# Attention of the x queries: steps of four heads, outputs of one unit beside the score gradients of the preceding unit, TensorE order fixed by hand

## Chip, core and metric

The kernel runs on one core of a Trainium2 chip. The metric is the device time of one execution in microseconds (us), as the median of several executions. The program before takes 9416.67 us (three executions, 9407.48 to 9422.91).

## The reference, cut to what matters

The program computes a forward value and eleven gradients of a gated mixture of two attention branches, `out = g*a + (1-g)*b`. Branch A is a 32-head attention of width 18 with one shared key and value. Branch B, in which the change lies, cuts 2048 tokens into 64 segments of 32; each segment attends to itself and to 8 memory rows, with 32 heads of width 128, and the first 8 output rows are the next segment's memory:

```python
for s in range(n_seg):
    xs = x[:, s * seg_len:(s + 1) * seg_len, :].copy()
    h = jnp.concatenate([mem, xs], axis=1)
    q = jnp.einsum('btd,dhe->bhte', h, Wq)
    ...
    scores = jnp.where(mask[None, None], scores, -1000000000.0)
    p = _softmax(scores, axis=-1)
    o = jnp.einsum('bhqk,bhke->bhqe', p, v)
    o = jnp.einsum('bhte,hed->btd', o, Wo)
    mem = o[:, :M, :].copy()
    outs.append(o[:, M:, :])
...
return g * a + (1 - g) * b
...
_out, _vjp = jax.vjp(_f, A_x, A_wq, ...)
_grads = _vjp(grad_out)
```

## The kernel before

The program works through stages, each of which opens and closes its own memory pools (`build_full`): branch A (`a_setup`, `a_attention`, `a_final`), the projections of all tokens (`b_project`), the serial forward chain of the memory rows (`b_chain_fwd`), the attention of the x queries (`b_x_attention`), the serial backward chain (`b_chain_bwd`), the gradients of x (`b_x_gradients`), and the gradients of the weights (`b_weight_gradients`). What one stage hands to a later one goes through DRAM.

`b_project` writes q, k and v twice: token by token (`XT`, tokens on partitions) and column by column (`XE`, the 128 elements of a head on partitions). In `XE` the heads of a half stand in the order i, g, where a head's number is 16 r + 4 g + i. For k and v it also writes `XS`, segment by segment (tile `p_seg`, copied on GpSimd).

`b_x_attention` is the stage of the change. It takes 16 tiles of 128 tokens (`tt`), and for each two halves of 16 heads (`r`): 32 units. For the 16 heads of a unit, with masks that keep each token to its own segment, it

- loads the key, query and value columns and rows (`x_ke`, `x_qe`, `x_ve`, `x_tv`, `x_tq`, `x_tk`, six transfers of 512 KB) and the memory columns (`x_me`, made on GpSimd of `raw_x_me`), and turns the latter into rows (`x_mk`, `x_mv`);
- takes the scores against the memory rows (L505 to L511: four heads share the array, each in 32 of its columns) and their exponentials `x_em` (ScalarE), then in four groups the scores against the tokens and the exponentials `x_et` (L519);
- sums them with one-column matmuls into `pl`, and takes the reciprocals `x_rl` on VectorE (L526);
- multiplies them with the values: for each head one matmul of all 128 rows with `x_tv`, and one of 32 rows (a quarter of the array) with `x_mv`, in turn (L532 to L535); VectorE scales the result to `x_ot` (L536), which is transposed to `x_oe` and projected with `WoN` into `pb`;
- makes the gradients of the outputs from `dbT` and `WoT` (`x_dot`, transposed to `x_doe`), in five matmuls, the last of which has 64 rows; multiplies them with `x_oe` on GpSimd (`x_pr`, L560);
- makes the gradients of the scores, `x_dsm` for the memory rows and `x_dst` for the tokens (L576, VectorE);
- transposes `x_et`, `x_dst`, `x_em` and `x_dsm` (`x_eq`, `x_sq`, `x_eqm`, `x_sqm`), sums over the memory rows (`x_dk`), and makes the gradients of the queries (`x_dq`): again one matmul of 128 rows with `x_tk` and one of 32 rows with `x_mk`, in turn (L604 to L606).

Every result goes back to DRAM in six transfers of 512 KB, three from the queue of SyncE (SP) and three from that of GpSimd (POOL), and eight small ones of `x_dk`. `pb` collects the projections of both halves of a token tile, and the tile ends with the gate's work on 576 columns (`x_bs`, `x_diff`, `x_out`, `dz_all`) and two one-row matmuls for the gradient of the gate.

The order of the instructions on each engine is set by a list scheduler, which may move them past each other; where `self.chain` is true, `follow` (L66) ties each TensorE instruction to the one before, and TensorE keeps the order in which the code is written. In this stage `chain` is false. Matmul results go into one pool of banks, `x_p` with four buffers, transposes into `x_tr` with two, `pb` takes two banks. Every matmul is recorded at L78 and every transpose at L83, inside the helpers `mm` and `tr`; copies out of transposes are at L62 (VectorE) or L64 (ScalarE).

Of the kernel before, what the change touches and what calls it, by code (L numbers as in the profile page):

```python
# [11 lines left out]
P = 128  # L12
# [17 lines left out]
class Kern:  # L30
# [3 lines left out]
    def __init__(self, tc, T, A_x, A_wq, A_wk, A_wv, A_wo, B_mem0, B_Wq, B_Wk, B_Wv, B_Wo,  # L34
# [19 lines left out]
        self.chain, self.last = False, None  # L54

# [158 lines left out]
    def b_project(self, keep, sp, psum):  # L214
# [6 lines left out]
        for tt in range(NTT):  # L221
            tok = slice(tt * P, (tt + 1) * P)
            for w in "kvq":
                tk = sp.tile([P, J], BF16, name="p_tok", bufs=2)
                te = sp.tile([P, 2, 4, 4, P], BF16, name="p_em", bufs=2)
                for c in range(8):
                    pb = psum.tile([P, 512], F32, name="p_pb", bufs=4)
                    for kt in range(NKT):
                        wap, rows = self.w_nat(w, kt, c * 512, (c + 1) * 512)
                        self.mm(pb[:, :], lhsT=xT[rows, kt, tok], rhs=wap, start=(kt == 0), stop=(kt == NKT - 1))  # L230
                    self.evac(tk[:, c * 512:(c + 1) * 512], pb[:, :])
                    ptr = psum.tile([P, 4, P], BF16, name="p_tr", bufs=3)
                    for i in range(4):
                        self.tr(ptr[:, i], tk[:, c * 512 + i * E:c * 512 + (i + 1) * E], P)
                    self.evac(te[:, c // 4, :, c % 4, :], ptr[:])
                nc.sync.dma_start(self.XT[w][tok, :], tk[:, :])
                nc.gpsimd.dma_start(self.XE[w][tt], te[:].rearrange("p r i g t -> p (r i g t)"))
                if w == "q":
                    continue
                for sl in range(4):  # L240
                    ts = sp.tile([P, 32, SEG], BF16, name="p_seg", bufs=2)
                    nc.gpsimd.tensor_copy(ts[:], te[:].rearrange("p r i g (s t) -> p (r i g) s t", s=4)[:, :, sl, :])
                    nc.gpsimd.dma_start(self.XS[w][4 * tt + sl], ts[:].rearrange("p h t -> p (h t)"))
# [162 lines left out]
    def load_WoT(self, pool, psum, WoN):  # L406

        t = pool.tile([P, NKT, J], BF16, name="WoT")
        for h4 in range(8):
            for kt in range(NKT):  # L410
                rows = KT_ROWS[kt]
                ptr = psum.tile([P, 4, P], BF16, name="x_tr", bufs=2)
# [7 lines left out]
    def load_em(self, sp, name, src, tt, r, bufs=2):  # L420

        t = sp.tile([P, 4, 4, P], BF16, name=name, bufs=bufs)
        self.nc.sync.dma_start(t[:].rearrange("p i g t -> p (i g t)"), src[tt][:, r * 2048:(r + 1) * 2048])
# [21 lines left out]
    def tr4(self, psum, name, src_fn, dst, use=None):  # L445

        ptr = psum.tile([P, 4, P], BF16, name="x_tr", bufs=2)
# [4 lines left out]
    def b_x_attention(self, keep, sp, psum, WoN, WoT):  # L452


        nc = self.nc
        NTT = self.NTT
        gwb = keep.tile([P, D], BF16, name="gwb")
        nc.sync.dma_start(gwb[:], self.gate_w.partition_broadcast(P))
        pdgs = keep.tile([1, D], F32, name="dgate_acc")
        for tt in range(NTT):  # L460
            tok = slice(tt * P, (tt + 1) * P)
            x = sp.tile([P, D], BF16, name="x_x", bufs=2)
            nc.sync.dma_start(x[:], self.A_x[tok, :])
            go = sp.tile([P, D], BF16, name="x_go", bufs=2)
            nc.sync.dma_start(go[:], self.grad_out[tok, :])
            at = sp.tile([P, D], BF16, name="x_a", bufs=1)
            nc.sync.dma_start(at[:], self.a_dram[tok, :])
            zc = sp.tile([P, 4], F32, name="x_z", bufs=2)
# [7 lines left out]
            gt, omg = zc[:, 2:3], zc[:, 3:4]  # L476
            db = sp.tile([P, D], BF16, name="x_db", bufs=2)
            nc.vector.tensor_scalar(out=db[:], in0=go[:], scalar1=omg, scalar2=None, op0=ALU.mult)
            nc.gpsimd.dma_start(self.db_dram[tok, :], db[:])
            dbT = sp.tile([P, NKT, P], BF16, name="x_dbT", bufs=2)  # L480
            for k4, n in ((0, 4), (4, 1)):
                ptr = psum.tile([P, 4, P], BF16, name="x_tr", bufs=2)
                for k in range(n):
                    rows = KT_ROWS[k4 + k]
                    self.tr(ptr[0:rows, k, :], db[:, (k4 + k) * P:(k4 + k) * P + rows], P)
                rows = KT_ROWS[k4]
                self.evac(dbT[0:rows, k4:k4 + n, :], ptr[0:rows, 0:n, :])
            pb = psum.tile([P, 640], F32, name="x_b", bufs=1)
            for r in range(2):
                qe = self.load_em(sp, "x_qe", self.XE["q"], tt, r)  # L490
                ke = self.load_em(sp, "x_ke", self.XE["k"], tt, r)
                ve = self.load_em(sp, "x_ve", self.XE["v"], tt, r, 1)
                hc = slice(r * 2048, (r + 1) * 2048)
                xt = {}
                for w in "vqk":
                    xt[w] = sp.tile([P, 4, 4, E], BF16, name=f"x_t{w}", bufs=1)
                    nc.sync.dma_start(xt[w][:].rearrange("p g i e -> p (g i e)"), self.XT[w][tok, hc])
                me = self.load_me(sp, "x_me", self.ME, (1, 2), tt, r)
                mk = self.tok_me(sp, psum, "x_mk", me, 0)
                mv = self.tok_me(sp, psum, "x_mv", me, 1)  # L500
                mes = lambda w, i, g: me[:, w, 4 * i + g, :]

                et = sp.tile([P, 4, 4, P], BF16, name="x_et", bufs=1)
                em = sp.tile([P, 4, P], BF16, name="x_em", bufs=1)
                Sm = psum.tile([P, 4, P], F32, name="x_p", bufs=4)  # L505
                self.mm(Sm[:].rearrange("p i n -> p (i n)"), lhsT=self.identB[:, :],
                        rhs=self.maskM[:].rearrange("p i n -> p (i n)"), start=True, stop=False)
                for i in range(4):
                    for g in range(4):
                        self.mm(Sm[32 * g:32 * g + 32, i, :], lhsT=mes(0, i, g), rhs=qe[:, i, g, :],  # L510
                                start=False, stop=True, tp=(0, 32 * g))  # L511
                nc.scalar.activation(em[:], Sm[:], ACT.Exp, scale=SCALEB)
                for i in range(4):
                    S = psum.tile([P, 4, P], F32, name="x_p", bufs=4)
                    self.mm(S[:].rearrange("p g n -> p (g n)"), lhsT=self.identB[:, :],
                            rhs=self.maskX[:].rearrange("p g n -> p (g n)"), start=True, stop=False)
                    for g in range(4):
                        self.mm(S[:, g, :], lhsT=ke[:, i, g, :], rhs=qe[:, i, g, :], start=False, stop=True)
                    nc.scalar.activation(et[:, i], S[:], ACT.Exp, scale=SCALEB)  # L519
                pl = psum.tile([P, 4, 4], F32, name="x_p", bufs=4)  # L520
                for i in range(4):
                    self.mm(pl[:, i, :], lhsT=em[:, i, :], rhs=self.selG[:, :], start=True, stop=False)
                    for g in range(4):
                        self.mm(pl[:, i, g:g + 1], lhsT=et[:, i, g, :], rhs=self.onesB[:, :], start=False, stop=True)
                rl = sp.tile([P, 4, 4, 1], F32, name="x_rl", bufs=2)
                nc.vector.reciprocal(rl[:, :, :, 0], pl[:, :, :])  # L526
                ot = sp.tile([P, 4, 4, E], BF16, name="x_ot", bufs=1)
                oe = sp.tile([P, 4, 4, P], BF16, name="x_oe", bufs=1)
                for g in range(4):
                    rs = slice(32 * g, 32 * g + 32)  # L530
                    po = psum.tile([P, 4, E], F32, name="x_p", bufs=4)
                    for i in range(4):  # L532
                        self.mm(po[:, i, :], lhsT=et[:, i, g, :], rhs=xt["v"][:, g, i, :], start=True, stop=False)
                        self.mm(po[:, i, :], lhsT=em[rs, i, :], rhs=mv[rs, i, :],
                                start=False, stop=True, tp=(32 * g, 0))  # L535
                    nc.vector.tensor_tensor(out=ot[:, g], in0=po[:], in1=rl[:, :, g, :].to_broadcast([P, 4, E]), op=ALU.mult)  # L536
                    self.tr4(psum, "x_tr", lambda i: ot[:, g, i, :], oe[:, :, g, :])
                nc.gpsimd.dma_start(self.OX[tok, hc], ot[:].rearrange("p g i e -> p (g i e)"))
                for i in range(4):
                    for g in range(4):  # L540
                        h = 16 * r + 4 * g + i
                        st, sp_ = r + i + g == 0, r == 1 and i + g == 6
                        self.mm(pb[:, 0:512], lhsT=oe[:, i, g, :], rhs=WoN[:, h, 0:512], start=st, stop=sp_)
                        self.mm(pb[:, 512:D], lhsT=oe[:, i, g, :], rhs=WoN[:, h, 512:D], start=st, stop=sp_)

                dot = sp.tile([P, 4, 4, E], BF16, name="x_dot", bufs=1)
                doe = sp.tile([P, 4, 4, P], BF16, name="x_doe", bufs=1)
                for g in range(4):
                    c = 4 * r + g
                    pd = psum.tile([P, 4, E], F32, name="x_p", bufs=4)  # L550
                    for kt in range(NKT):
                        rows = KT_ROWS[kt]
                        self.mm(pd[:].rearrange("p i e -> p (i e)"), lhsT=dbT[0:rows, kt, :],
                                rhs=WoT[0:rows, kt, c * 512:(c + 1) * 512], start=(kt == 0), stop=(kt == NKT - 1))
# [1033 lines left out]
```

## Time and profile before

| what | value |
|---|---|
| median of three executions | 9416.67 us |
| the profiled execution | 9416.26 us, its span 9414.5 us |
| mean granted clock of TensorE over the span | 0.909 |
| TensorE busy (matmuls) | 8638.8 us, 92% of the span |
| VectorE, ScalarE, GpSimd busy | 4330.9, 3805.1, 1282.8 us |
| stage of the change, about | 4963 to 6492 us, 1529 us of the span |

Durations are in us from the start of the span, unless marked ns. A matmul's row has its start, its duration to the end of its drain, and its shape; as matmuls are pipelined, the distance of two starts, not the duration, is what one costs. In the view of stretches the column PEclk is the granted clock (1.00 is full speed), and the DMA share is the busy share of 16 DMA engines. In the view of waits, a row says which engine's instruction waited for what.

### The profile page before, as it was taken

What the parts mean: (1) busy time and instruction counts of PE and PEld (TensorE: products, weight loads), DVE (VectorE), ACT (ScalarE), POOL (GpSimd) and SP (SyncE); (2) the same over time, 40 slices, a digit from 0 to 9 for tenths busy, and PEclk for the clock granted to TensorE, in tenths of its full rate; (3) what the DMA queues carried; (4) which work ended last, traced back from release to release, by engine and by line L of the source; (5) the groups of instructions that cost most, each with busy time, mean ns of one, the idle gap of its engine ahead of it and who ended that gap; (6) DMA issues with size and microseconds to landing.
All of it is one profiled execution on the core that took longest, in us unless ns stands there. A gap on an engine that the chain in (4) does not pass through costs nothing. (4 is left out here: it accounts for less than half of the span.)

```text
span 9414.5 us, 208637 instructions
## 1 busy us (share of the span) xinstructions
PE 8638.8 (92%) x89432; PEld 4097.2 (44%) x89432; DVE 4330.9 (46%) x6561; ACT 3805.1 (40%) x7316; POOL 1282.8 (14%) x3014
## 2 busy tenths in 40 slices
PE   7999999999999799799998888886999989997999
PEld 2222222222222344355555555554777745554444
DVE  4889889889889344233333333332222211113000
ACT  3877778778778333222222222222222211112000
POOL 4000000000000133100002222221000011112000
PEclk9999999999999899799997777777999977776999
DMA  2000000000000355411125444444333366666444
GB/s 83 1 5 5 1 5 5 1 5 1 5 1 1 132 231 232 174 59 60 59 72 187 158 157 157 160 153 182 99 99 96 93 212 188 185 189 208 164 150 141
DMA packets 559619, 969.71 MB, mean 103 GB/s; under 512 B 184473, under 2 KB 371106, under 8 KB 538530
## 3 DMA queue, kind: packets, MB, share of 16 engines
q1 hardware_dynamic: 493362, 705.87, 23.5%
q0 software_dynamic: 64016, 249.18, 7.0%
q8 instruction: 699, 11.45, 0.5%
q14 instruction: 230, 1.88, 0.1%
q10 hardware_dynamic: 1312, 1.33, 0.0%
HBM read 552.06 MB, written 404.10 MB: 102 GB/s over the span
## 5 line engine op out<-in xcount | busy, mean ns | idle before, releaser
L1216 DVE TENSOR_TENSOR a_U<-a_d,a_E 128x1024 bf16<-128x1024 f32 x2048 | 2474.5, 1224 | 298.2 <-ACT a_E L1211 229.4
L1211 ACT ACTIVATE a_E<-a_s 128x512 bf16<-128x512 f32 x4096 | 2237.5, 595 | 561.8 <-PE a_s L78 475.8
L78 PE MATMUL a_s<-a_qaug,a_kmask 128*128 128x512 bf16 x2048 | 701.4, 386 | 54.7 <-ACT a_tk L1293 24.5
L78 PE MATMUL a_s<-a_kmask,a_qaug 128*128 128x512 bf16 x2048 | 698.6, 384 | 25.9 <-ACT a_E L1211 9.6
L78 PE MATMUL w_acc<-w_col,w_h 128*128 128x512 bf16 (+1 forms) x2400 | 525.2, 380 | 11.2 <-DMA w_col<-dqx 11.2
L78 PEld LDWEIGHTS <-d_g 128*32 128x32 bf16 x18432 | 494.7, 97 | 33.9 <-issue 18.0
L62 DVE CAST p_tok<-p_pb 128x512 bf16<-128x512 f32 x384 | 265.4, 692 | 318.2 <-PE p_pb L78 318.2
L78 PE MATMUL a_d<-a_doT,a_vaugT 32*128 32x512 bf16 x2048 | 400.0, 387 | 0.0
L78 PE MATMUL a_d<-a_vaugT,a_doaT 32*128 32x512 bf16 x2048 | 398.2, 386 | 0.0
L1303 POOL TENSOR_TENSOR a_otok<-a_tk,a_rl 128x144 bf16<-128x144 f32 x64 | 27.5, 429 | 2518.8 <-DVE a_rl L1302 2518.8
L64 ACT COPY p_em<-p_tr 128x512 bf16<-128x512 bf16 x384 | 225.0, 586 | 357.7 <-PE p_tr L83 357.5
L78 PEld LDWEIGHTS <-w_h 128*128 128x128 bf16 (+1 forms) x2400 | 237.1, 100 | 299.5 <-issue 33.6
L78 PEld LDWEIGHTS <-a_vaugT 32*128 32x128 bf16 x2048 | 96.3, 91 | 570.3 <-issue 570.3
L78 PEld LDWEIGHTS <-a_doaT 32*128 32x128 bf16 x2048 | 95.9, 91 | 539.3 <-issue 538.8
L64 ACT CAST c_tm<-c_pb 128x512 bf16<-128x512 f32 x192 | 112.5, 586 | 472.8 <-PE c_pb L78 472.6
L912 ACT ACTIVATE g_dt<-x_p 128x512 bf16<-128x512 f32 x256 | 142.7, 599 | 353.1 <-PE x_p L78 194.6
L62 DVE CAST c_tm<-c_pb 128x512 bf16<-128x512 f32 x192 | 132.9, 692 | 313.5 <-PE c_pb L78 309.1
L78 PEld LDWEIGHTS <-c_mT 128*32 128x32 bf16 x7680 | 187.9, 96 | 190.9 <-DVE c_mT L394 25.4
L62 DVE CAST w_o<-w_acc 128x512 bf16<-128x512 f32 (+1 forms) x60 | 41.4, 690 | 491.6 <-PE w_acc L78 467.1
L78 PEld LDWEIGHTS <-a_kmask 128*128 128x128 bf16 x2048 | 124.8, 97 | 312.0 <-issue 304.1
L78 PEld LDWEIGHTS <-p_xT 128*128 128x128 bf16 (+1 forms) x1920 | 154.8, 97 | 217.9 <-issue 87.6
L78 PE MATMUL x_b<-WTq,g_dqe 128*128 128x512 bf16 (+1 forms) x1024 | 200.7, 360 | 43.1 <-DMA g_dqe<-dqe 43.1
(484 smaller groups left out, 14443.7 us busy)
## 6 DMA issues: line engine op xcount, KB each, us to landing
xt_k<-p_tok SPq DMA_DIRECT2D x16, 1024.0 KB, 3.9
xe_k<-p_em POOLq DMA_DIRECT2D x16, 1024.0 KB, 5.3
xs_k<-p_seg POOLq DMA_DIRECT2D x64, 256.0 KB, 3.7
xt_v<-p_tok SPq DMA_DIRECT2D x16, 1024.0 KB, 4.2
xe_v<-p_em POOLq DMA_DIRECT2D x16, 1024.0 KB, 5.9
xs_v<-p_seg POOLq DMA_DIRECT2D x64, 256.0 KB, 3.7
xt_q<-p_tok SPq DMA_DIRECT2D x16, 1024.0 KB, 4.6
xe_q<-p_em POOLq DMA_DIRECT2D x16, 1024.0 KB, 5.8
```

The lines of the kernel that those rows point to most:

```text
L62: nc.vector.tensor_copy(out, in_)
L64: nc.scalar.copy(out, in_)
L78: self.follow(self.nc.tensor.matmul(out, lhsT, rhs, start=start, stop=stop, tile_position=tp, skip_group_check=True))
L912: nc.scalar.mul(dt[:, g], pk[:], sc)
L1211: nc.scalar.activation(ex[:, j, :], s[:, :], ACT.Exp, scale=SCALEA)
L1216: nc.vector.tensor_tensor(out=u[:], in0=d[:], in1=ex[:], op=ALU.mult)
L1303: nc.gpsimd.tensor_tensor(out=osl, in0=v[:, :, :, o0:o0 + DA], in1=rl[:].to_broadcast([P, 4, 2, DA]), op=ALU.mult)
```

## The change

The whole stage is written anew, and its TensorE order is fixed by hand (`self.chain = True`). In the shortened lines below `B` is the unit whose outputs are made, `C` the preceding unit, whose score gradients and what follows from them are made, `N` the next one. The loop has 33 passes of four steps; step g takes the four heads of one g.

- A step's TensorE order is: scores of B, score gradients of C, transposes of C's last `dq`, output gradients of B, sums of B, projection of B's last outputs, outputs of B, transposes of C's `dst`, query gradients of C, transposes of C's `et`, of B's `ot` and of B's `dot`. The work on memory rows stands in single steps (in step 0 `memory_gradients`, in 1 and 2 `memory_sums`, in 2 `memory_columns`, in 3 `memory`).
- In `two_parts` the four matmuls of 128 rows come first, then the four of 32 rows, where the kernel before takes them in turn. `dbT` and `WoT` are padded with zeros, so that the fifth matmul has 128 rows too.
- Tiles are cut: loads and stores are halves of 256 KB (2 KB for each partition instead of 4), `x_dst`, `x_oe` and others hold one step. `XE`, `EQ`, `SQ` and `DQE` have the heads in the order g, i; `b_project`, `load_em` and `b_x_gradients` follow that (for `p_seg` with two copies in place of one).
- `x_pr` is computed on VectorE instead of GpSimd. All 12 stores of a unit are issued by GpSimd, none by SyncE; the eight small stores of `x_dk` become two, issued by SyncE.
- `x_p` has three buffers instead of four, `x_tr` three instead of two. Copies out of transposes have a set engine: `x_oe`, `x_eq`, `x_dqe` on ScalarE, `x_sq`, `x_doe` on VectorE.
- The gradient of the gate's weights is taken in `b_weight_gradients`, in 32 one-row matmuls.

```diff
+        def two_parts(out, lt, rt, lm, rm, g):
+            rs = slice(32 * g, 32 * g + 32)
+            for i in range(4):
+                self.mm(out[:, i, :], lhsT=lt(i), rhs=rt(i), start=(i == 0), stop=False)
+            for i in range(4):
+                self.mm(out[:, i, :], lhsT=lm[rs, i, :], rhs=rm[rs, i, :], start=False, stop=True, tp=(32 * g, 0))
...
+        self.chain = True
...
+        for k in range(len(units) + 1):
...
+                if B:
+                    if g > 1:
+                        loads_second(B, g - 2)
+                    scores(B, g)
+                if C:
+                    score_gradients(C, g)
+                for fn in late:
+                    fn()
+                late = []
+                if B:
+                    output_gradients(B, g)
+                if C and g == 0:
+                    memory_queries(C, "em")
+                    out_project(C, 3, C["oe"])
+                    if C["r"] == 1:
+                        take(C["tt"])
+                    memory_gradients(C)
+                if C and g == 1:
+                    memory_sums(C, 1, "dot", 1.0)
+                    memory_queries(C, "dsm")
+                if C and g == 2:
+                    memory_sums(C, 0, "tq", SCALEB)
+                    if C["r"] == 1:
+                        finish(C["tt"])
+                if B:
+                    sums(B, g)
+                    if g:
+                        out_project(B, g - 1, B["oe"])
+                    outputs(B, g)
...
+                if C:
+                    rows(C, "sq", g, C["dst"], self.SQ, "v")
+                    query_gradients(C, g)
+                    rows(C, "eq", g, at(C, "et", g), self.EQ, "s")
+                    late.append(lambda C=C, g=g: rows(C, "dqe", g, at(C, "dq", g), self.DQE, "s"))
+                if B:
+                    out_columns(B, g)
+                    gradient_columns(B, g)
```

On TensorE, at the end of a unit's query gradients before, the matmuls with `x_tk` (128 rows) and with `x_mk` (32 rows) stand in turn, each with its weight load, and the next unit's scores follow:

```order
L78 LDWEIGHTS x_dst
L78 MATMUL x_p<-x_tk,x_dst 128x128
L78 LDWEIGHTS x_dsm
L78 MATMUL x_p<-x_mk,x_dsm 128x128
L78 LDWEIGHTS identB
L78 MATMUL x_p<-maskM,identB 128x512
```

In the changed program the same place in a step of four heads has the last of the four matmuls with `x_tk`, and then the first two of the four with `x_mk`:

```order
L79 LDWEIGHTS x_dst
L79 MATMUL x_p<-x_tk,x_dst 128x128
L79 LDWEIGHTS x_dsm
L79 MATMUL x_p<-x_mk,x_dsm 128x128
L79 LDWEIGHTS x_dsm
L79 MATMUL x_p<-x_mk,x_dsm 128x128
```

The four of 32 rows now follow each other, as do the four of 128 rows before them; after them come the transposes of the same four heads' `x_et`, not a new unit.

On VectorE, the kernel before takes one kind of work of a whole unit after the other; from the last scaled output of a unit to its score gradients stand:

```order
L536 TENSOR_TENSOR x_ot<-x_p,x_rl 128x512 x2
L62 COPY x_oe<-x_tr 128x4x128
L555 TENSOR_TENSOR x_dot<-x_p,x_rl 128x512
L62 COPY x_doe<-x_tr 128x4x128
L555 TENSOR_TENSOR x_dot<-x_p,x_rl 128x512 x2
L62 COPY x_doe<-x_tr 128x4x128
L555 TENSOR_TENSOR x_dot<-x_p,x_rl 128x512
L62 COPY x_eq<-x_tr 128x512
L576 TENSOR_TENSOR x_dst<-x_p,x_et 128x512
L569 TENSOR_TENSOR x_dsm<-x_p,x_em 128x512
L576 TENSOR_TENSOR x_dst<-x_p,x_et 128x512 x3
```

In the changed program, from step 0 into step 1 of a pass, where `x_dst`, `x_dsm` and `x_sq` belong to the preceding unit and the others to the one whose outputs are made:

```order
L654 TENSOR_TENSOR x_dst<-x_p,x_et 128x512
L630 TENSOR_TENSOR x_dsm<-x_p,x_em 128x512
L566 RECIPROCAL x_rl<-x_p 128x4
L569 TENSOR_TENSOR x_dot<-x_p,x_rl 128x512
L583 TENSOR_TENSOR x_ot<-x_p,x_rl 128x512
L63 COPY x_sq<-x_tr 128x512
L63 COPY x_doe<-x_tr 128x512
L610 TENSOR_TENSOR x_pr<-x_doe,x_oe 128x512
L654 TENSOR_TENSOR x_dst<-x_p,x_et 128x512
```

Every step now has one of each, `x_pr` is among them, and in step 0 `x_dsm` stands ahead of the reciprocals and of `x_dot`.

388 lines of the change are left out of this document (227 added, 161 removed).

## The prediction, made before the changed kernel ran

> **What bounds the kernel now.** I read the page first, then the view of stretches for the stage of the change and two stages beside it, then the tile `x_et`, the waits and the order of time inside the stage.
>
> From the page: the span, and its 40 slices of 235 us with the busy tenths of TensorE and its granted clock.
>
> ```profile
> span 9414.5 us, 208637 instructions
> PE   7999999999999799799998888886999989997999
> PEclk9999999999999899799997777777999977776999
> ```
>
> The view of stretches: `b_project`, the stage of the change, `b_x_gradients`.
>
> ```profile
> core 0: us, PE busy (x) PEld busy (x) DVE busy (x) ACT busy (x) POOL busy (x), PEclk, DMA share, GB/s
> 3268.00:3850.00 582.00, 580.37 (x3466) 245.52 (x3465) 266.19 (x386) 226.26 (x386) 221.03 (x304) 1.00 0.57 229
> 4963.00:6492.00 1529.00, 1337.58 (x11383) 780.26 (x11383) 513.30 (x1047) 435.40 (x779) 430.10 (x766) 0.75 0.47 156
> 7575.00:8582.00 1007.00, 960.51 (x7967) 519.08 (x7967) 162.28 (x352) 179.84 (x320) 166.33 (x480) 0.77 0.61 192
> ```
>
> In the stage of the change TensorE is busy for 1337.58 of 1529 us, VectorE and ScalarE for a third, the DMA engines for 0.47. So TensorE bounds it, and in two ways at once: it idles for 191 us, and its clock is 0.75, whereas `b_project`, as busy, has 1.00. The tiles `x_et` and `x_dqe` give the period of a unit and the end of the stage.
>
> ```profile
> L519 ACT ACTIVATE x_et<-x_p x128: 589/598/616, 4960.2 to 6447.4; 128x512 bf16<-128x512 f32 x128
> L64 ACT COPY x_dqe<-x_tr x64: 586/586/587, 5007.4 to 6490.8; 128x512 bf16<-128x512 bf16 x64
> ```
>
> From the first exponentials of the first unit to the last of the 32nd are 1487.2 us; less about 5 us inside a unit and over 31 periods, that is 47.8 us a unit. The stage ends at 6491.4, 1531 us after 4960.2. The view of waits says what TensorE's matmuls wait for, and the timeline of one unit where:
>
> ```profile
> PE x_p L78 <- POOL x_pr L560: 91.1, 107, 3.7
> PE x_tr L83 <- ACT x_sq L64: 38.0, 95, 0.7
> ```
>
> ```profile
> 5757.50 0.25 PE L78 MATMUL x_p<-x_pr,negonesB 128*32 128x128 bf16 x4 [1.73 <-POOL x_pr L560]
> 5758.61 0.25 PE L78 MATMUL x_p<-x_pr,negonesB 128*32 128x128 bf16 x4 [0.48 <-POOL x_pr L560]
> ```
>
> The largest wait, 91.1 us, is for the products on GpSimd; the next for copies out of the two transpose buffers. The rest of the loss is the clock. Three stretches of one unit:
>
> ```profile
> 5718.50:5725.40 6.90, 5.07 (x70) 3.60 (x69) 1.93 (x7) 3.91 (x7) 2.01 (x4) 0.99 0.89 289
> 5725.40:5735.60 10.20, 10.20 (x72) 5.88 (x73) 1.48 (x4) 4.32 (x8) 3.40 (x7) 0.50 0.63 204
> 5735.60:5742.40 6.80, 6.80 (x72) 4.41 (x71) 2.07 (x5) 2.06 (x4) 0.00 (x0) 1.00 0.61 215
> ```
>
> In the second TensorE is busy all the time and has half its clock. What it does there, and at full clock before it, are mostly the matmuls of 128 and 32 rows in turn:
>
> ```profile
> 5723.41 0.23 PE L78 MATMUL x_p<-x_mk,x_dsm 32*128 32x128 bf16 x1
> 5723.57 0.23 PE L78 MATMUL x_p<-x_tk,x_dst 128*128 128x128 bf16 x1
> 5723.73 0.22 PE L78 MATMUL x_p<-x_mk,x_dsm 32*128 32x128 bf16 x1
> 5725.98 0.29 PE L78 MATMUL x_p<-x_tk,x_dst 128*128 128x128 bf16 x1
> 5726.20 0.28 PE L78 MATMUL x_p<-x_mk,x_dsm 32*128 32x128 bf16 x1
> ```
>
> Their starts are 0.16 us apart at full clock and 0.22 at half. Other work goes faster:
>
> ```profile
> 5736.20 0.38 PE L78 MATMUL x_p<-maskX,identB 128*128 128x512 bf16 x1
> 5736.42 0.39 PE L78 MATMUL x_p<-x_qe,x_ke 128*128 128x128 bf16 x4
> ...
> 5763.11 0.39 PE L83 MATMUL x_tr<-identB,x_dst 128*128 128x128 bf16 x4
> 5763.34 0.39 PE L83 MATMUL x_tr<-identB,x_et 128*128 128x128 bf16 x4
> 5764.22 0.38 PE L83 MATMUL x_tr<-identB,x_dst 128*128 128x128 bf16 x4 [0.49 <-ACT x_sq L64]
> ```
>
> **The change part by part.** Four matmuls or transposes of 128 columns cost 0.23 us (5763.11 to 5763.34), 0.057 each, so one in the alternation loses 0.10 us. The array's use says more: a pair in turn takes 0.32 us for one matmul's worth of 0.057 and a quarter of another, about a fifth of what the array could do, and the half clock follows such stretches and waits. I take it that dense work keeps the clock full, as `b_project`'s 1.00 says.
>
> TensorE's work in a unit of the changed program, at full clock. First, groups of four of 128 columns: nine a step (`dq`, `dst`, `et`, `ot`, `dot` transposed; `ke`, `ve`, `tv`, `tk`), 36 a unit, and 4.6 for `em`, `dsm`, `me` and `db`: 40.6 x 0.23 = 9.3 us. Second, 29 of 512 columns (20 of the output gradients, 9 of masks and minus ones); 0.22 us each (5736.20 to 5736.42): 6.4 us. Third, 16 pairs with `WoN`, 512 and 64 columns:
>
> ```profile
> 5746.79 3.35 PE L78 MATMUL x_b<-WoN,x_oe 128*128 128x512 bf16 x26
> 5722.47 0.55 PE L78 MATMUL x_p<-x_sqm,x_tq 128*128 128x32 bf16 x16 [0.73 <-ACT x_sqm L64]
> 5722.86 0.55 PE L78 MATMUL x_p<-x_eqm,x_dot 128*128 128x32 bf16 x16
> ```
>
> 26 in 3.35 us are 0.26 a pair: 4.1 us. Fourth, the 32 matmuls of 32 rows, now in eight groups of 0.23, with 16 changes of shape at 0.10: 3.4 us. Fifth, the small ones: 32 of 32 columns take 0.39 us for 16, 0.8 us; 32 one-column sums at the same 0.024 each, 0.8 us; 16 and 32 on quarters of the columns, between 0.014 (four at once) and 0.057 each, I take 0.03, and four changes: 1.9 us. The sum is 26.7 us; the last matmul's drain in the row of 26 adds some 0.2 to it, so 26.5. The same sum for the kernel before has 64 in turn at 0.16 where now stand 64 in 16 groups and 16 changes: 10.2 in place of 5.3; and eight changes for the fifth matmul with its 64 rows, 0.8. That gives 32 us. From the trace: 47.8 us x 0.75 = 36 us of full clock, less 6 us idle (191 over 32) at some clock between 0.5 and 1, leaves 30 to 33. So the sum holds.
>
> The clock: at 26.5 us of work within some 30 us the array has work of full columns most of the time, and I expect 0.95 to 1.0. [...]
>
> What is left is waiting, hand-off by hand-off. The durations:
>
> ```profile
> L555 DVE TENSOR_TENSOR x_dot<-x_p,x_rl 128x512 bf16<-128x512 f32 x128 | 88.1, 688 | 50.9 <-PE x_p L78 50.8
> L560 POOL TENSOR_TENSOR x_pr<-x_doe,x_oe 128x512 bf16<-128x512 bf16 x128 | 149.2, 1191 | 11.6 <-issue 10.9 <-ACT x_doe L64 0.7
> L64 ACT COPY x_sq<-x_tr 128x512 bf16<-128x512 bf16 x128 | 75.1, 586 | 252.1 <-PE x_tr L83 252.1
> L62 DVE COPY x_eq<-x_tr 128x512 bf16<-128x512 bf16 x128 | 54.3, 424 | 81.4 <-PE x_tr L83 80.6
> ```
>
> VectorE's `x_pr` is not in the trace; bounds are its copies of that size, 0.42, and its products from matmul banks, 0.69. I take 0.45, nearer to the copy since both operands are bf16. A step on VectorE: three products of 0.69, a reciprocal (0.26 now, for 16 columns; under 0.2 for four), two copies and `x_pr`: 3.6 us. ScalarE: five of 0.6, 3.0 us. A step of TensorE is 5.5 to 6.8 us, so neither bounds it. From a group's start to the one that needs its copy, 5763.11 to 5764.22, are 1.11 us: 0.39 for the matmuls, 0.586 for the copy, so 0.13 for both hand-offs.
>
> In step g=1 to 3 I find every result needed ready in time or within 0.35 us: exponentials of ScalarE are needed 1.7 us after the scores, `x_ot` 1.1 us after the outputs and takes 0.23 + 0.69 + 0.07. Step 0 is different. `memory_gradients` takes a bank between output gradients and sums, so with three banks the outputs get the bank of the output gradients, which `x_dot` must have emptied; and VectorE does `x_dsm` first. After the sums come 0.7 us left of `x_dsm`, 0.2 of reciprocals, 0.69 of `x_dot` and the hand-offs, and no projection stands between: 1.7 us of wait. Steps 1 and 2, with a bank for `memory_sums`, have the same tie, but 1 us of projection covers all but 0.2. The work at the ends of token tiles stands in VectorE's queue too (`x_out` waits for GpSimd's `x_diff`, 1.28 us): 0.8 us every second unit. Sum of waits: 1.7 + 0.4 + 0.4 + 0.4 + 0.6 for short ones = 3.5 us. A unit takes 26.5 + 3.5 = 30 us.
>
> The old waits go: for `x_pr` because its reader is a pass later, for transposes because of the third buffer and the mixed order. GpSimd, busy for 430 of the 1529 us, loses 4 x 1.19 us and eight small stores a unit and gains nine stores; of what it makes only `x_me` and `x_diff` are waited for, and `x_me` two steps later.
>
> Transfers: the queues' view for 5140 to 6280.
>
> ```profile
> q1 hardware_dynamic: 63984, 126.49, 34.9%
> q0 software_dynamic: 17032, 51.95, 12.3%
> ```
>
> 47.2% of 47.8 us are 22.6 us of all 16 engines for a unit; with rows of 2 KB instead of 4 a little more, say 24. In 30 us they fit at 0.8, and a half is asked for at least two steps, 11 us, ahead.
>
> The stage: a first pass of 20 us (no score gradients, so nothing fills the waits), 31 passes of 30, a last of 16: 966 us; for the two end passes together I would not exclude 25 to 50. Against 1531 that is 565 us less. Elsewhere: the 32 one-row matmuls of the gate cost 16 x 0.26 = 4 us or nothing, where TensorE waits for the weight stage's first transfer; the split copy of `p_seg` is hidden, as GpSimd is busy for 221 of 582 us there and TensorE bounds that stage. I add 4. So 9416.3 - 565 + 4 = 8855 us; the profiled execution is 0.4 us from the median, so no correction.
>
> **The rivals.** *The hand-offs cost more.* Each step waits some 1.3 us more, because VectorE or ScalarE, each with a strict queue, comes late once and shifts the next, or because transfers at 0.8 arrive late. For it: slack of 0.1 to 0.4 us at most hand-offs, and no stage of the kernel before runs its transfers at 0.8. Against it: single lateness is caught up over a step, as VectorE and ScalarE have 2 us to spare. A unit of 34 to 36 us, stage 1090 to 1150: 8980 to 9040.
>
> *The clock stays.* With a mean of 0.75, 26.5 / 0.75 + 3 = 38 us a unit, the stage 31 x 38 + 36 = 1214: 9103. For it: `b_x_gradients`, with 95% busy, has 0.77. Against it: that stage keeps the matmuls in turn, which go here. [...]
>
> *Slower: the half clock holds itself.* At half clock the changed stream uses the array at most at half, and the row 5725.40 shows that full occupation alone does not bring the clock back. If it falls in step 0's wait and stays, work takes 53 us a unit, the stage about 31 x 53 + 40 = 1683 and the kernel 9570. It decides from a mean clock under 0.6. Against it: the clock came back at 5735.60 after denser work than the alternation, and a step has over 2 us of such.
>
> *Better.* VectorE gets to step 0's `x_dot` earlier and the short waits vanish, so that only 1 us is left: 27.5 us a unit, 8778.
>
> That the change doesn't do what it says is excluded by the order on the engines, as shown above.
>
> **How the numbers follow.** Forecast (28 to 32 us a unit, 8793 to 8917): 0.56. More hand-offs (to 9040): 0.2. Better (under 8793): 0.12. Clock stays: 0.09. Half clock holds: 0.03. The range goes from 27.3 us a unit in the better case to 35.3 in the worse, 8770 to 9020, which leaves out the clock cases and the tips of two others, about 0.19. A measurement of this kernel can tell 0.2%, 19 us, from no change; all cases but one are far below. Faster 0.96, same 0.01, slower 0.03.
>
> **What would show it.** Right: the period of `x_et` near 30 us, PEclk over 0.95 in the stage, starts of `x_tk` matmuls 0.057 apart, no wait for `x_pr`, and the largest wait of TensorE in the outputs of step 0, for `x_dot`. Wrong: a granted clock under 0.9; a wait for DMA above 1 us a unit; waits for ScalarE's `x_et` or VectorE's `x_ot` in every step; a change outside the stage of over 10 us.

## The result, and the profile after

The changed kernel takes 8815.22 us (median of four executions, 8803.35 to 8827.08); the kernel before, beside it, 9412.08 (9406.64 to 9422.91). The ratio is 0.9365, with a 95% interval of 0.9348 to 0.9381. The profiled execution took 8803.35 us. From its page, the span and the 40 slices, now of 220 us:

```profile
span 8801.6 us, 210293 instructions
PE   6999999999999979978999899979999799997999
PEclk9999999999999989979999999989999877776999
```

The view of stretches, for the stage of the change and the gradients of x (columns as before: length, busy time of five engines, granted clock, DMA share, GB/s):

```profile
4963.00:5885.00 922.00, 847.14 (x11700) 587.42 (x11700) 512.59 (x1143) 464.83 (x875) 304.62 (x673) 0.98 0.80 259
...
6970.00:7980.00 1010.00, 961.96 (x7975) 520.18 (x7976) 164.31 (x361) 179.84 (x320) 169.34 (x489) 0.77 0.61 192
```

The stage has 922 us where it had 1529, its clock is 0.98 instead of 0.75, and TensorE idles for 75 us instead of 191. The gradients of x, which still take matmuls of 128 and 32 rows in turn, have 0.77 as before. The tiles `x_et` and `x_dqe` give the period:

```profile
L552 ACT ACTIVATE x_et<-x_p x128: 597/627/628, 4974.8 to 5869.7; 128x512 bf16<-128x512 f32 x128
L65 ACT COPY x_dqe<-x_tr x128: 586/587/617, 5001.8 to 5887.2; 128x512 bf16<-128x512 bf16 x128
```

From the first step's exponentials to the last step's of the 32nd unit are 894.9 us, 31.75 periods: 28.2 us a unit, against 47.8. From the first `x_et` to the last copy of `x_dqe` the stage takes 913 us (1531 before). What TensorE's matmuls still wait for, between 5000 and 5860, or 30.5 units (total, times, longest):

```profile
PE x_tr L84 <- ACT x_eq L65: 20.1, 30, 0.9
PE x_tr L84 <- DVE x_ot L583: 16.2, 24, 0.9
PE x_p L79 <- DVE x_dsm L630: 15.8, 30, 0.5
PE x_p L79 <- DVE x_rl L566: 6.3, 9, 2.2
```

Together 58.4 us, or 1.9 a unit, all for copies and products of VectorE and ScalarE; `x_pr` is not among them. No matmul waits for a load itself, but VectorE does: in its queue the next token tile's `x_db` stands ahead of this unit's work until its load is there:

```profile
DVE x_db L488 <- DMA x_go<-in_grad_out_dram: 25.2, 14, 3.7
```

Each of the nine waits for `x_rl` comes right behind one of these. The timeline of a step 0 at the end of a token tile shows the waits for `x_dsm` and `x_ot`:

```profile
5423.28 0.69 DVE L630 TENSOR_TENSOR x_dsm<-x_p,x_em 128x512 bf16<-128x512 f32 x1 [2.26 <-PE x_p L79]
...
5424.03 0.38 PE L79 MATMUL x_p<-x_tv,x_et 128*128 128x128 bf16 x4 [0.53 <-DVE x_dsm L630]
5424.77 0.82 DVE L686 SCALAR_TENSOR_TENSOR x_out<-x_diff,x_z,x_bs 128x576 bf16<-128x576 f32 x1 [0.71 <-POOL x_diff L684]
5425.51 0.69 DVE L569 TENSOR_TENSOR x_dot<-x_p,x_rl 128x512 bf16<-128x512 f32 x1
...
5426.85 0.40 PE L84 MATMUL x_tr<-identB,x_ot 128*128 128x128 bf16 x4 [0.90 <-DVE x_ot L583]
```

The outputs start 0.06 us after `x_dsm` ends (5423.28 + 0.69) and 1.48 us before `x_dot` begins. So the bank that they wait for is the one that `x_dsm` empties, not that of `x_dot`. Behind it VectorE waits 0.71 us for GpSimd's `x_diff`, does the tile's `x_out`, and is late with `x_ot`.

### The profile page after: what moved, and what is told of

Same layout as the page of the kernel before. It is cut to its first block, busy times and chain, and to the rows that moved or that the text cites. A ratio compares the mean times of both kernels' runs of the same rounds, so it can differ in the third digit from the quotient of the medians.

```text
span 8801.6 us, 210293 instructions
## 1 busy us (share of the span) xinstructions
PE 8158.4 (93%) x89816; PEld 3903.5 (44%) x89816; DVE 4321.7 (49%) x6659; ACT 3835.0 (44%) x7412; POOL 1184.8 (13%) x3062
## 5 line engine op out<-in xcount | busy, mean ns | idle before, releaser
L65 ACT CAST w_o<-w_acc 128x512 bf16<-128x512 f32 (+1 forms) x60 | 35.1, 585 | 496.6 <-PE w_acc L79 496.6
```

The lines of the kernel that those rows point to most:

```text
L65: nc.scalar.copy(out, in_)
```

## The experiments

Theory A: most of the gain is a denser stream on TensorE. Grouping saves changes of shape, the other unit's work fills the waits, and the half clock goes with stretches that use little of the array, as in the 10.20 us at 0.50 before (from 5725.40). Against it stood: a change of shape itself brings the clock down; the waits do; the fixed order alone carries the gain. Each ratio is to executions of the kernel before taken beside that kernel, whose medians were 9402 to 9416 us; differences of 20 us or less are better read from the ratios than from the medians. All kernels:

| kernel | median us | ratio to before, 95% interval | us a unit in the stage | clock there |
|---|---|---|---|---|
| before | 9412.08 | | 47.8 | 0.75 |
| before, grouped | 9153.55 | 0.9723 (0.9707 to 0.9739) | 39.5 | 0.86 |
| the same, `x_pr` on VectorE | 9084.23 | 0.9649 (0.9634 to 0.9663) | 37.5 | 0.87 |
| changed | 8815.22 | 0.9365 (0.9348 to 0.9381) | 28.2 | 0.98 |
| changed, in turn | 8980.46 | 0.9538 (0.9524 to 0.9552) | 33.4 | 0.95 |
| changed, free order | 8840.67 | 0.9391 (0.9377 to 0.9405) | 29.6 | 0.95 |
| changed, `x_p` 4 and `x_tr` 2 buffers | 8972.46 | 0.9530 (0.9516 to 0.9545) | 33.4 | 0.91 |
| changed, fifth matmul of 64 rows | 8825.55 | 0.9384 (0.9369 to 0.9400) | 29.1 | 0.99 |
| changed, `x_pr` on GpSimd | 8808.83 | 0.9371 (0.9357 to 0.9385) | 28.4 | 0.97 |
| changed, projection later | 8810.04 | 0.9370 (0.9356 to 0.9384) | 28.5 | 0.95 |
| changed, dense work added to the gradients of x | 8923.97 | 0.9479 (0.9465 to 0.9493) | | |
| changed, gradients of x grouped | 8700.79 | 0.9243 (0.9229 to 0.9257) | | |
| the same, two buffers of `g_dt` | 8539.87 | 0.9081 (0.9067 to 0.9094) | | |
| the same, gate work held back | 8517.43 | 0.9049 (0.9034 to 0.9064) | 28.1 | 0.98 |

**The kernel before, grouped.** The same edit in the outputs and in the query gradients:

```diff
                     for i in range(4):
-                        self.mm(po[:, i, :], ..., start=True, stop=False)
+                        self.mm(po[:, i, :], ..., start=(i == 0), stop=False)
+                    for i in range(4):
                         self.mm(po[:, i, :], lhsT=em[rs, i, :], rhs=mv[rs, i, :],
```

> The kernel before, in which only the matmuls of 128 and of 32 rows are grouped by four instead of taken in turn, in the outputs and in the query gradients. Theory A (grouping saves work, and the granted clock follows how densely the array is used over a few us): work of a unit falls from 32 to 27 us at full clock, the stretches of alternation that stood at half clock vanish, the clock of the stage rises from 0.75 to 0.85 or more, the 6 us of waits stay; 27 / 0.9 + 6 = 36 us a unit instead of 47.8, the kernel at 9040 to 9110 us. Rival R1 (the clock falls because of the waits and the copies' pauses, not of the alternation): clock stays about 0.75, 27 / 0.75 + 6 = 42 us a unit, the kernel at 9230. Rival R2 (the new order is everything): under 50 us gained, 9360 or more.

It gained 259 us, between theory A's 300 to 370 and R1's 180. The stage, and three stretches of a unit around the wait for `x_pr`:

```profile
4963.00:6236.00 1273.00, 1043.57 (x11256) 651.14 (x11383) 513.93 (x1049) 424.05 (x778) 431.25 (x770) 0.86 0.56 189
...
5612.00:5618.90 6.90, 4.48 (x29) 1.98 (x29) 3.00 (x6) 1.17 (x2) 1.57 (x2) 1.00 0.15 57
5619.30:5622.70 3.40, 2.34 (x35) 1.11 (x30) 0.57 (x1) 0.00 (x0) 3.04 (x3) 0.51 0.01 1
5622.70:5625.90 3.20, 3.20 (x27) 2.46 (x23) 2.79 (x5) 0.34 (x1) 1.95 (x8) 0.50 0.00 0
```

The half clock now comes behind a stretch in which TensorE is busy for only 4.48 of 6.90 us, stays while it is busy for 2.34 of 3.40 (0.51), and goes on for 3.20 us in which it is busy throughout (0.50). Theory A overrated how much of the half clock lay in the alternation: with no pair in turn left the clock of the stage is 0.86, and some of the half clock stands beside the waits.

**The same, with `x_pr` on VectorE.** `nc.gpsimd.tensor_tensor` becomes `nc.vector.tensor_tensor` in the line that makes `pr`.

> The kernel before, grouped by four (9153.6 us), with x_pr on VectorE in place of GpSimd. It tells how much of the rest of the gain is the old wait for x_pr, and how much needs the second unit beside the first. Theory A (the wait for x_pr was GpSimd's slow product in a strict order of kinds): most of its 91 us go, the clock of the stage rises from 0.86 to 0.90 or so, 39.5 us a unit become 35 to 36, the kernel at 9010 to 9060. Rival (in the old order VectorE is as late, since x_dot and the copies stand before it; the wait only changes its name): 9110 to 9160.

It gained 69 us more, between the two. The waits of the grouped kernel, 5000 to 6200, and of this one, 5000 to 5860:

```profile
PE x_p L78 <- POOL x_pr L561: 90.9, 120, 3.7
PE x_tr L83 <- ACT x_sq L64: 34.7, 87, 0.7
```

```profile
PE x_tr L83 <- ACT x_sq L64: 28.9, 57, 0.8
PE x_p L78 <- DVE x_pr L561: 16.9, 23, 0.9
```

For each unit (30.4 in the first stretch, 22.9 in the second) the wait for `x_pr` falls from 3.0 to 0.7 us; those for transposes stay, and so does the clock (0.87). The remaining 269 us to the changed kernel come with the rest of the change.

**The changed kernel, in turn.**

```diff
             for i in range(4):
-                self.mm(out[:, i, :], lhsT=lt(i), rhs=rt(i), start=(i == 0), stop=False)
-            for i in range(4):
+                self.mm(out[:, i, :], lhsT=lt(i), rhs=rt(i), start=True, stop=False)
                 self.mm(out[:, i, :], lhsT=lm[rs, i, :], rhs=rm[rs, i, :], start=False, stop=True, tp=(32 * g, 0))
```

> The changed kernel with the matmuls of 128 and 32 rows in turn again (four pairs instead of two groups of four), all else as changed. Eight groups a unit go from some 0.62 to 1.28 us: 5.3 us of work a unit. Theory A: the stretches in turn are 1.3 us long and stand between dense work, so the clock stays at 0.93 or more, the unit goes from 28.2 to 33 or 34 us, the kernel to 8960 to 9000 us. Rival R3 (the change of shape itself brings the half clock down, wherever it stands): clock about 0.8, unit (26.3 + 5.3) / 0.8 + 2 = 41 us, the kernel at 9200 or more.

```profile
4963.00:6060.00 1097.00, 1021.92 (x11561) 676.52 (x11721) 518.87 (x1144) 465.13 (x878) 307.44 (x681) 0.95 0.68 217
```

165 us more, the unit 5.2 us longer, the clock 0.95: as theory A has it. R3 falls. Here, with dense work beside it, a change of shape cost about its 0.10 us (48 of them a unit, 5.2 us) and left the clock nearly alone (0.95 for 0.98). In this order grouping is worth 165 us, in the old one 259, since there it also raised the clock, from 0.75 to 0.86.

**Free order.** Without `self.chain = True` in the stage.

> The changed kernel with the order on TensorE in the stage left to the scheduler, as everywhere before; code, tiles, banks and groups as changed. Theory A (the order matters only through the waits it leaves): unit 29 to 32 us, clock 0.9 or more, the kernel at 8840 to 8950. Rival R4 (the fixed order carries the gain): the scheduler moves the kinds of work apart again, waits of 5 us or more a unit, clock 0.85 or less, unit 36 us or more, the kernel above 9050.

It took 25 us more. R4 falls: the order fixed by hand is worth 0.3%, and the scheduler, given code written by steps, finds nearly the same. TensorE's waits are few and long, nearly all for one product, and what held VectorE before it was a load:

```profile
PE x_p L79 <- DVE x_dst L654: 62.5, 14, 6.9
```

```profile
DVE x_db L488 <- DMA x_go<-in_grad_out_dram: 80.0, 14, 8.2
```

`x_db` now stands further ahead in VectorE's queue: before each of the 14 waits for `x_dst` the queue has `x_db` with its wait, `x_doe`, `x_pr` and only then `x_dst`. So even these 25 us may come from its place there and not from TensorE's order; the two weren't tried apart.

**Four matmul banks, two transpose buffers.**

```diff
-        bank = lambda shape, dt=F32: psum.tile(shape, dt, name="x_p", bufs=3)
+        bank = lambda shape, dt=F32: psum.tile(shape, dt, name="x_p", bufs=4)
...
-                k.ntr = 3
+                k.ntr = 2
```

> The changed kernel with x_p in four buffers and x_tr in two, as before, all else as changed. Theory A (the outputs of step 0 wait for the bank that x_dot empties; the third transpose buffer is what keeps the transposes from waiting for copies): the waits for x_dsm and x_rl in step 0 vanish (0.7 us a unit), but in every step the transposes of x_dot find their buffer still full of x_et's, 0.6 us each, 2 to 3 us a unit; the kernel at 8850 to 8900. Rival (either is slack, the copies are done in time): 8790 to 8825.

157 us more, about twice what theory A gave. The waits between 5000 and 5860:

```profile
PE x_tr L84 <- ACT x_eq L65: 38.2, 69, 1.1
PE x_tr L84 <- DVE x_ot L583: 31.3, 26, 1.6
PE x_tr L84 <- ACT x_oe L65: 18.2, 25, 0.7
PE x_tr L84 <- ACT x_mv L65: 16.8, 25, 0.7
```

Those for `x_dsm` and `x_rl` are gone, as expected, but transposes now wait 104.5 us in these four rows, where the changed kernel has 36.3, and the clock falls to 0.91 with it, which the expectation left out. The run changes two numbers at once; as it takes a bank's wait away and still loses, the third transpose buffer is one of the larger parts of the change, by argument and not by a run of its own.

**The fifth matmul with 64 rows.** `lhsT` and `rhs` of the output gradients are cut to `[0:KT_ROWS[kt]]` again.

> The changed kernel without the padding: the fifth matmul of the output gradients has 64 rows again. Theory A (a change of shape costs 0.10 us, two of them a step): 0.2 x 4 x 32 = 26 us more, the kernel at 8830 to 8850, clock unchanged. Rival (a matmul of half the rows among four full ones costs nothing, or the change is hidden): within 10 us of 8815.

The medians differ by 10 us, the ratios by 0.0019, or 18 us, with intervals that overlap; so the time alone doesn't tell. The trace does: here, and then in the changed kernel, the five matmuls and what follows them:

```profile
5427.18 1.35 PE L79 MATMUL x_p<-WoT,x_dbT 128*128 128x512 bf16 x5
5428.46 0.40 PE L84 MATMUL x_tr<-identB,x_em 128*128 128x128 bf16 x4
```

```profile
5420.20 1.24 PE L79 MATMUL x_p<-WoT,x_dbT 128*128 128x512 bf16 x5
5421.28 0.39 PE L84 MATMUL x_tr<-identB,x_em 128*128 128x128 bf16 x4
```

1.28 us from start to start against 1.08: two changes of shape, 0.10 us each, as the prediction had it, and 25.6 us over 128 steps. The period of `x_et`, 29.1 us (922.9 over 31.75), is 0.6 to 0.9 longer than in the four kernels whose stage is that of the changed one (894.9 to 902.5 us over the same 31.75 periods).

**`x_pr` on GpSimd in the changed kernel.** The line L610 with `nc.gpsimd`.

> The changed kernel with x_pr on GpSimd again, all else as changed; it had 8815 us. Theory A (with the reader of x_pr a pass later, the engine does not matter): no wait of TensorE for x_pr, VectorE 0.42 us lighter a step; the kernel within 20 us, 8795 to 8835. Rival R5 (the move to VectorE was needed, as GpSimd also issues all 12 stores and takes 1.19 us for one product): waits for x_pr return in step 0, where x_dsm needs the products of all four steps, 1 to 2 us a unit; the kernel at 8845 to 8880.

No difference (8808.83, the interval takes in the changed kernel's), and one wait for `x_pr` between 5000 and 5860:

```profile
PE x_p L79 <- POOL x_pr L610: 1.3, 1, 1.3
```

So the engine of `x_pr` does not matter once its reader is a pass later. In the old order, with its reader close behind, GpSimd's 1.19 us did matter: there the move to VectorE brought 69 us.

**The projection later.** In step 0 `out_project(C, 3, C["oe"])` and `take` stand between the sums and the outputs instead of ahead of `memory_gradients`.

> The changed kernel with the projection of the last x_oe of the preceding unit moved, in step 0, from ahead of the gradients of the memory rows to between the sums and the outputs, 1 us of matmuls; it had 8815 us. Theory A (the outputs of step 0 wait because their bank is the one that x_dot empties late): the wait for x_dsm and x_rl in step 0, 22 us over 30 units, and part of that for x_ot vanish; 0.5 to 0.9 us a unit, the kernel at 8785 to 8800. Rival (the wait only moves, as VectorE and not the place of a matmul is late): 8805 to 8825, with the wait named at another place.

The rival was right on the time: 8810.04, no difference. The waits for `x_dsm`, `x_rl` and `x_ot` vanish, and another takes their place; behind it stands VectorE's wait for a load, which was 25.2 us in the changed kernel:

```profile
PE x_p L79 <- DVE x_dst L654: 39.3, 15, 4.4
```

```profile
DVE x_db L488 <- DMA x_go<-in_grad_out_dram: 55.7, 14, 5.7
```

In 14 of the 15 waits `x_db`, with its wait, stands ahead of `x_doe`, `x_pr` and `x_dst` in VectorE's queue, as in free order. So VectorE is late, as the rival says, but because of the next tile's load, whose reader the scheduler moved further ahead in this kernel. What the move of the projection brings with `x_db` held back wasn't tried.

**Dense work added.** Is it the alternation or the emptiness of the array that halves the clock? In the gradients of x, whose matmuls stay in turn, three useless dense matmuls go ahead of each group of four pairs.

```diff
+                        for _ in range(3):
+                            self.mm(pk[:].rearrange("p i n -> p (i n)"), lhsT=self.identB[:, :],
+                                    rhs=lt[:, g].rearrange("p i n -> p (i n)"))
                         for i in range(4):
```

> The changed kernel (8815 us) with useless dense work in the stage of the gradients of x, whose matmuls of 128 and 32 rows stay in turn: ahead of each group of four pairs three matmuls of 128 rows and 512 columns, whose result the first matmul of the group overwrites. 8 x 3 x 0.22 = 5.3 us of work a unit, 169 us over 32 units at full clock. Theory A (the clock follows the share of the array that is in use over a few us: four pairs alone use about a fifth of it, with the added matmuls about half): the clock of the stage rises from 0.77 to 0.92 or more, which gives back all that the added work takes: 24.2 + 5.3 = 29.5 us of work a unit against 31.5 us now, the kernel at 8740 to 8850. Rival R3 (the alternation itself, a change of shape, holds the clock down): clock 0.80 or less, the added work costs 169 / 0.78, the kernel at 8980 to 9050.

```profile
6970.00:8081.00 1111.00, 1014.91 (x8575) 553.92 (x8735) 166.91 (x352) 183.22 (x320) 165.19 (x480) 0.94 0.56 171
```

```profile
7409.35 0.82 PE L79 MATMUL x_p<-g_eq,identB 128*128 128x512 bf16 x3
7410.01 0.22 PE L79 MATMUL x_p<-g_dot,g_eq 128*128 128x128 bf16 x1
```

The clock rises from 0.77 to 0.94, so R3 falls a second time. Three cost 0.66 us (7409.35 to 7410.01), 169 us over 256 groups, while TensorE is busy only 53 us longer (1014.91 against 961.96): the clock gave back 116. The kernel is still 109 us slower, where theory A expected it at 8740 to 8850. Two things were missed: matmuls in turn gain less than others from the full clock, since they are 0.16 us apart there and 0.22 at half, and 46.7 us of new waits came up for `g_dt`, whose one buffer its store holds.

**The gradients of x grouped.** The same split of the pairs into two loops there.

> The changed kernel with the same grouping by four also in the loop of the key and value gradients of the stage of the gradients of x, which has the two kinds in turn and a clock of 0.77. Eight groups in each of 32 units: 5.3 us of work a unit less, about 24 us of work at full clock in 31.5 us now. Theory A: the clock of that stage goes from 0.77 to 0.95 or more, its unit to 21 to 25 us, its length from 1010 to 700 to 800 us, unless its transfers into single buffers (0.61 of the DMA engines now) bind first, which would leave it at 800 to 850; the kernel at 8510 to 8650. Rival R1: the clock stays near 0.77, unit 31.5 - 5.3 / 0.77 = 24.6 us with a clock of 0.77, the kernel near 8600. Rival R2: no change over 50 us.

```profile
6970.00:7870.00 900.00, 720.51 (x7877) 434.02 (x7971) 167.83 (x353) 179.62 (x320) 166.18 (x480) 0.90 0.65 216
```

```profile
PE x_tr L84 <- ACT g_dt L1043: 124.0, 31, 6.0
```

```profile
ACT g_dt L1043 <- DMA dvx<-g_dt: 259.6, 32, 10.3
```

114 us gained, and no expectation met: the kernel was to come to 8510 to 8650. TensorE's busy time fell by 241 us (961.96 to 720.51) and the clock rose to 0.90, but a wait of 124 us came up, as `g_dt` has one buffer and ScalarE writes it only when its store has left. The expectation had looked at the loads.

**Two buffers of `g_dt`.** `bufs=1` becomes `bufs=2`.

> The kernel with the grouping also in the stage of the gradients of x (8700.8 us), and two buffers in place of one for g_dt there, whose store held TensorE for 124 us of that stage's 900. Theory A: without that wait the stage takes 22.5 us a unit or less and its clock rises from 0.90 to 0.97 or more: 700 to 775 us, the kernel at 8500 to 8580. Rival (the transfers bind: 0.65 of the DMA engines over 900 us would be 0.80 over 730, and the five loads go into single buffers): TensorE then waits for a load, stage 800 or more, the kernel at 8600 to 8680.

```profile
6970.00:7710.00 740.00, 671.92 (x7871) 411.68 (x7967) 166.05 (x352) 189.85 (x320) 165.88 (x480) 0.97 0.80 262
```

161 us more, 152 by the ratios: the wait goes, and with it most of the half clock that was left (0.97 for 0.90). The rival falls: the transfers take 0.80 of the DMA engines, and behind the stage's first load TensorE waits for loads only 0.5 us. From 1010 us the stage came to 740.

**The gate's work held back.** `prepare` of the next token tile is made to follow the TensorE instruction written before it, which sets only its place in the order.

> The kernel grouped in both stages with two buffers for g_dt (8539.9 us), and the work on the next token tile's gate kept out of the queues of VectorE and ScalarE until the pass that needs it: in the changed kernel ScalarE's x_z of tile 1 stands ahead of the first x_em and waits for a load until 4973.69, while the scores were there at 4958.3. Theory A (that wait delays the first pass): first x_et at 4955 to 4962 in place of 4971 to 4975, 8 to 15 us less, the kernel at 8524 to 8532. Rival (the first pass waits for its own loads anyway): within 4 us of 8540.

The start of the stage in the changed kernel, and the tile `x_et` here:

```profile
4973.69 0.20 ACT L483 ACTIVATE x_z<-x_z 128x1 f32<-128x1 f32 x1 [17.78 <-DVE x_z L481]
...
4974.26 0.60 ACT L542 ACTIVATE x_em<-x_p 128x512 bf16<-128x512 f32 x1
```

```profile
L556 ACT ACTIVATE x_et<-x_p x128: 597/630/631, 4955.0 to 5847.4; 128x512 bf16<-128x512 f32 x128
```

22 us gained, 30 by the ratios, more than the 8 to 15 expected: the first exponentials come at 4955.0, and the waits for `x_rl`, before which `x_db` had stood in VectorE's queue with a wait for a load, are gone too. This version, 8517.43 us, beats both kernels (0.9049 of before).

## Why the prediction was right, point by point

*TensorE's work, 26.5 us a unit: right.* 28.2 less 1.9 of waits are 26.3. The price of a change of shape, 0.10 us, came out at 0.10 in the kernel with 64 rows, and the kernel in turn puts back 48 changes a unit for 5.2 us, 0.11 each with the little that its clock adds.

*The clock, 0.95 to 1.0: right,* with 0.98. That dense work keeps it full was an assumption then; with dense work added, the clock of the gradients of x went from 0.77 to 0.94. The rival "the clock stays" fell. So did "the half clock holds itself": in the changed kernel, behind the first pass, the half clock came in six stretches of 3.4 us (5369.5 to 5372.9 is one), each of them followed by full clock (length, TensorE's busy time, granted clock, DMA share, GB/s):

```profile
5366.00:5369.40 3.40, 2.30 (x40) 1.00 0.61 208
5369.50:5372.90 3.40, 3.13 (x23) 0.50 0.34 90
5372.90:5376.30 3.40, 3.40 (x50) 1.00 0.79 208
```

*The waits, 3.5 us a unit: mis-sized,* they are 1.9. The step that failed is the wait in the outputs of step 0, put at 1.7 us. It was derived from a bank that `x_dot` must empty; it is the bank of `x_dsm`, one reciprocal and one product earlier on VectorE, and it costs 0.52 (15.8 us over 30.5 units). So the sign "the largest wait in the outputs of step 0, for `x_dot`" did not come. What the prediction saw coming at the end of token tiles is there, for `x_ot`, 0.5 a unit against 0.4. The largest wait, for `x_eq`, 0.7 a unit, is one that its working doesn't name; only the 0.6 for short waits could hold it. Of the sum's three terms of 0.4 the working gives the source of two. And the load in VectorE's queue, behind the 0.2 a unit for `x_rl`, isn't in it: it looked at the loads of the matmuls alone.

*`x_pr` on VectorE, 0.45 us: right* (0.426 in the middle), and no wait for it. It goes "because its reader is a pass later", as the prediction says: on GpSimd the kernel is as fast, so the move to VectorE adds nothing here.

*The transfers, 24 us of all DMA engines a unit: a little too much.* They took 22.6 (0.80 of 28.2 us), as much as the 22.6 before; that rows of 2 KB take more than those of 4 was an estimate, and did not show.

*The old waits for transposes go "because of the third buffer and the mixed order": right in the main.* The wait for `x_sq`, 38.0 us before, is gone, but those for `x_eq` and `x_ot` stand in its place with 36.3 us in 30.5 units. Without the third buffer (and with a fourth bank) 157 us come back, without the fixed order 25.

*The ends, 36 us, and elsewhere +4.* The end passes took 39 (913 less 31 x 28.2). Not foreseen: the first `x_et` is 14.6 us later than before, because ScalarE's queue has the next tile's `x_z` ahead of it. What follows the stage is 9.3 us shorter in the profiled execution; over the profiled kernels of this study whose later stages are those of the changed one it is 2913 to 2921 us, against 2923 before, so some of this is scatter. Altogether 9416.3 - 618 + 14.6 - 9.3 = 8803.4, the profiled execution's time. The forecast of 8855 was 40 us above the median. It had 1.8 us too much in each of 31 passes, 56 us, and 13 behind the stage, which came out 9.3 shorter where it had 4 more; against that stand the late start, 14.6, and 3 for the end passes, and the median is 12 above the profiled execution. That it came so close is thus in part luck: the late start hid a quarter of the 56.

*What carries the gain.* Of 597 us the grouping alone brings 259 in the old order and the move of `x_pr` 69 more. The other 269 come with the steps of four heads and all that goes with them; the third transpose buffer belongs here, and padding is worth 18 to 26. The parts don't simply add up: in the changed order the grouping is worth 165 and the move of `x_pr` nothing. How the rest divides between one unit beside the other and the cut tiles wasn't tried apart.

## What to carry to other kernels

Group matmuls by shape, even where the pairs belong to the same sum: a change cost 0.10 to 0.11 us here, and grouping alone took the clock of the stage from 0.75 to 0.86. The half clock went on into work that leaves no gap: in the kernel before, grouped, 3.20 us in which TensorE was busy throughout ran at 0.50, behind a stretch with waits. When a stage gets faster, look at what still has one buffer: in the gradients of x the store of `g_dt` took back more than half of what grouping gave, until a second buffer released it. Look in every engine's queue for work of the next tile that waits for a load ahead of work that is due: here `x_db` and `x_z` held VectorE and ScalarE so, and holding them back gained about as much as the fixed order did. And before fixing an order by hand, write the code in the wanted steps and let the scheduler do it: here that gave all but 0.3%.

## What the runs showed of the hardware

A clock well under 1.00 came without idle time too: in the gradients of x of the changed kernel it is 0.78 over these 920 us, in which TensorE's only wait is one of 0.2 us:

```profile
7020.00:7940.00 920.00, 917.01 (x7594) 495.84 (x7594) 153.54 (x336) 171.15 (x305) 160.89 (x464) 0.78 0.61 188
```

The same stage in five kernels:

| gradients of x | length, us | TensorE busy, us | granted clock |
|---|---|---|---|
| before, in turn | 1007 | 960.51 | 0.77 |
| changed, in turn | 1010 | 961.96 | 0.77 |
| changed, in turn, dense work added | 1111 | 1014.91 | 0.94 |
| changed, grouped | 900 | 720.51 | 0.90 |
| the same, two buffers of `g_dt` | 740 | 671.92 | 0.97 |

So in this stage the clock did not go with the share of time in which TensorE is busy: 0.95 of the time gave 0.77, 0.80 of the time 0.90. It rose to 0.94 when dense work was added while the pairs stayed in turn. That is one experiment with one amount of such work; how little of it would do was not tried.
